# A transformer block on one core: fillers by a running count, last weights behind attention outputs, two more quads on VectorE, LayerNorm priorities

## The chip, the core and the metric

The kernel runs on one core of a Trainium2 chip. The core has five engines with an instruction stream each: TensorE (PE in the profile, its weight loads PEld), VectorE (DVE), ScalarE (ACT), GpSimd (POOL) and SyncE (SP), which here issues nearly all DMAs. The streams meet only at semaphores, and each engine takes its instructions in order. The metric is the device time of one execution in microseconds (us). Lower is better.

## The reference

One adaptive LayerNorm block over 2048 tokens of width 640: attention with 32 heads of width 20, then a gated product network of width 1536. All inputs are bf16.

```python
mod = (_silu(c) @ w_mod).reshape(c.shape[0], 6, 1, -1)
sa, ca, ga, sb, cb, gb = ...
h = _layernorm(x) * (1 + ca) + sa
x = x + ga * _A_ref(h, A_wqkv, A_wo)      # softmax(q k^T / sqrt(20)) v, 32 heads, then wo
h = _layernorm(x) * (1 + cb) + sb
x = x + gb * _B_ref(h, B_w_gate, B_w_up, B_w_down)   # ((h wg) * (h wu)) wd
```

The scores are 32 matrices of 2048 x 2048, so 134 million exponentials are taken.

## The kernel before

**A planner.** The Python code does not write the engines' programs by hand. It makes tasks (class `Task`) with an engine, an estimated duration, dependencies and a priority, plays them through an event loop (`Sched.run`, `step_engine`, `pick_pe`) and writes each engine's instructions in the order in which that loop started them. `emit_program` then adds the semaphore waits. The estimates therefore decide only the *order*; on the chip an instruction waits for its semaphores, and everything behind it on its engine waits too. A DMA's estimated landing is computed in `finish_issue`: bytes at `DMA_RATE_2` = 240 per ns, then `DMA_LAT` 1700 ns, `DMA_SLOW` 0.0015 ns per byte, and after 60 us `DMA_MARGIN`, unless the transfer is `firm`.

**Tiling.** Queries are cut into six chunks (`CHUNKS`: 512, 512 and four of 256). In each chunk eight items of four heads follow each other. The scores of an item are cut into units of 128 partitions x 512 columns; a head uses 32 rows of TensorE's array, so four heads run side by side (L1502). Most units go in groups of two through ScalarE's exponential (L1539) into the `PP` ring. The others are computed by VectorE, four units at a time, a *quad*: four evictions that write the score as bits of a bf16 (L1563), two masks (L1595, L1603) and a product on VectorE (L1600) or in four pieces on GpSimd (L1615). A quad's result has two terms, so its units pass twice through the product with V (L2165). `QUADS` says how many quads each item of each chunk has, 104 in all.

**End of an item** (`item_end_tasks`). The accumulated product is transposed by VectorE (L1695), a reciprocal is taken (L1700), the product with it (L1702) runs on GpSimd, a second VectorE transpose writes `OcT` (L1711), and DMAs on SP's queue place it in `Ocp` (L1723). `ENDP` is the priority of these VectorE steps for a chunk's last item; `END3` decides whether that item's product runs on VectorE.

**After a chunk** (`suffix(ci)`), beside the next chunk's attention: output projection from `Ocp` (`wo,Ocp`, L952; added to x at L1804), second LayerNorm (statistics L1821 and L1823 on VectorE, L1824 and L1826 on GpSimd, normalisation L1828), transposes of its result (L1866) with eviction into `h2T` (L1871), twelve rounds of gate and up (`h2T,stg`) with their product (L1932, L1939), and the down projection (`wd,hprod`, added at L2035). All these have lower standing on TensorE than scores. The LayerNorm steps have priority `LN2P` on VectorE, where smaller goes first: evictions have 1, a quad's evictions 0.8. The last chunk's suffix has nothing behind it to run beside: it is the tail. Its matmuls use the whole array (L948, L1844).

**FFN weights** come by DMA (L1907), gate and up 160 KB each for 128 of the 1536 columns. For the first five chunks they go through three buffers `stg`, in turn. For the last chunk, ten of the twelve pairs have buffers of their own (`stx`) in space that the queries held; the first `nsq` pairs wait for the last score of the fifth chunk (`sfx_done["qdead"]`), the others for the fourth chunk's leftovers (`first`).

**The running count.** `activity(t, area)` notes each matmul group's work, a transpose like any other matmul (2.37 units per ns of estimated duration). `recent(t)` is the sum over the last `HAM_W` = 3413.3 ns. `roll` sums the same work over windows that start at multiples of `HAM_W`; where one has less than `HAM_MIN` = 2550, `cold` is set, and `clk()` doubles TensorE's estimated durations.

**What TensorE does next** (`pick_pe`): scores, if they can go; else, with little recent work, other work ahead of its turn; else products with V; else other work; else a filler. The lines that the change touches:

```python
if sc.recent(t) < FILL_MIN and ring() >= RINGLOW and pick_x(t, True):
    return True
if sc.recent(t) < FILL_HARD and t > 20000 and do_fill(t):
    return True
```

A filler (`do_fill`, L2498) is four matmuls of 32 x 512 columns of the identity into a free PSUM bank; it needs such a bank, and its result is not used. `STAGE` holds thresholds of these choices by item.

Of the kernel before, what the change touches and what calls it, by code (L numbers as in the profile page):

```python
# [130 lines left out]
class Sched:  # L131

    def __init__(self):
        self.tasks = []
        self.order = {k: [] for k in ("sp", "act", "pe", "dve", "pool")}
        self.all = []
        self.free_at = {k: T0 for k in self.order}
        self.pend = {k: [] for k in self.order}
        self.readyl = {k: [] for k in self.order}
        self.t = 0.0  # L140
        self.n = 0
        self.progress = 0
# [5 lines left out]
        self.ham_w = 0  # L148
        self.ham_act = 0.0
# [12 lines left out]
        self.lk_last = None  # L162
# [45 lines left out]
        heapq.heappush(self.pend[task.eng], (t, task.seq, task))  # L208

    def roll(self, t):  # L210
        w = int(t // HAM_W)
        while self.ham_w < w:
            self.cold = self.ham_act < HAM_MIN
            if self.cold:
                self.ncold += 1
            self.ham_act = 0.0
            self.ham_w += 1

    def activity(self, t, area):
        self.roll(t)  # L220
        self.ham_act += area
        self.hist.append((t, area))
        self.acts.append((t, area))

# [121 lines left out]
def emit_program(nc, sched, nsem_dma=56):  # L346
# [121 lines left out]


CHUNKS = ((0, 512), (512, 512), (1024, 256), (1280, 256), (1536, 256), (1792, 256))  # L470
QUADS = ((0, 4, 3, 3, 3, 4, 4, 4), (3, 5, 2, 4, 3, 4, 4, 4), (2, 1, 2, 1, 2, 1, 2, 1), (2, 1, 2, 1, 2, 1, 2, 1), (2, 2, 1, 2, 2, 2, 1, 2), (2, 1, 2, 2, 2, 1, 2, 0))
SPLITJ = 1
QHALF = ((0, 0), (0, 0))
TB_GATE = 2
# [75 lines left out]
NTERM = 2  # L550

STAGE = {
    0: {"FILL_MIN": 4190.746, "D_LATE": 16, "HOLD": 95, "PVMIN": 2, "XBACK": 0, "PVMAX": 14, "PVCAP": 12, "STEAL_GAP": 200, "XDPRIO": 1.343, "PVTOL": 249, "D_RES": 74, "LKTOL": 300.0, "EAGER": 9, "PV_KEEP": 2, "X_HALF": 0.0, "X_LATE": -179.96, "TPRIO": 0.75},
    1: {"FILL_MIN": 4712.6, "PV_KEEP": 2, "LKTOL": 200.7},
    2: {"DL": 0.376, "PVMAX": 4},
    3: {"HOLD": 124.6},
    5: {"STEAL_GAP": 310.6, "X_HALF": -32.3, "HOLD": 67.9},
    7: {"DL": 0.501, "D_RES": 40, "D_LATE": 17, "STEAL_GAP": 186.7},
    8: {"PV_KEEP": 3, "LKTOL": 0},
    9: {"X_HALF": -45.3},  # L560
    10: {"PVMIN": 1, "PV_KEEP": 3, "X_HALF": 68.7, "X_LATE": 186.7, "D_LATE": 21},
    11: {"DL": 0.443, "EAGER": 4, "FILL_MIN": 3731.3, "X_HALF": 38.6},
    12: {"DL": 0.459},
    13: {"DL": 0.417, "PVCAP": 17, "X_LATE": 44.2},
    15: {"D_RES": 41, "D_LATE": 22, "X_LATE": -177.3},
    16: {"X_LATE": -8.0, "EAGER": 6},
    19: {"DL": 0.471, "FILL_MIN": 4603.8, "XBACK": 0, "EAGER": 5},
    20: {"DL": 0.391, "HOLD": 136.1},
    21: {"XBACK": 0, "X_LATE": -47.9, "PV_KEEP": 2},
    22: {"X_HALF": -100, "X_LATE": -44.0},  # L570
    23: {"STEAL_GAP": 63.5, "X_HALF": 45.7, "HOLD": 124.7},
    24: {"DL": 0.464},
    25: {"DL": 0.549},
    26: {"DL": 0.411, "X_LATE": 65.8, "PVMAX": 3, "EAGER": 8},
    27: {"DL": 0.473},
    29: {"HOLD": 38.5, "PVMIN": 2, "LKTOL": 11.4},
    30: {"D_RES": 7, "PVMAX": 4, "X_HALF": -29.6},
    31: {"X_LATE": -186.8, "X_HALF": 32.8, "HOLD": 130.6},
    32: {"EAGER": 5, "D_LATE": 14, "HOLD": 153.7, "LKTOL": 269.4},
    33: {"DL": 0.442, "XBACK": 4, "PV_KEEP": 1},  # L580
    34: {"X_LATE": 5.0},
    35: {"X_LATE": 15.7},
    36: {"DL": 0.524, "EAGER": 3},
    38: {"HOLD": 43.6},
    42: {"HOLD": 47.1, "XBACK": 0},
    45: {"EAGER": 9, "PVTOL": 185.1},
}
XHALF = 1
STG_G0, STG_G, XC_G = 12, -10, -20
# [12 lines left out]
def build_kernel(nc, A_x, A_wqkv, A_wo, B_x, B_w_gate, B_w_up, B_w_down, c, w_mod, out):  # L602
# [184 lines left out]
    def ring():  # L787
        return len(pPs[0].free) + len(pPs[1].free)
# [961 lines left out]
    def suffix(ci):  # L1750
# [112 lines left out]
        for k in range(0 if tail and SPLITJ else KD):  # L1863
# [13 lines left out]
            if tail and T_SPLIT:  # L1877
# [20 lines left out]
        for fc in range(FT):  # L1898
            use_x = tail and fc < nsx
            wbuf, dm = [], []  # L1900
            for w_, wv in enumerate((wgv, wuv)):
                cell = {}
                if use_x:
                    cell["t"] = stx[fc][:, w_, :, :]

                def f(e, wv=wv, fc=fc, cell=cell):
                    return e.dma_start(cell["t"], wv[:, :, fc * 128:(fc + 1) * 128])  # L1907
# [461 lines left out]
    def pick_pe(t):  # L2369
# [204 lines left out]
```

## Time and profile before

| what | value |
|---|---|
| runs | 812.86, 808.64, 812.66 us; median 812.66 |
| profiled execution | 814.7 us, span 812.9 us |
| mean granted TensorE clock | 0.991 |
| VectorE masks L1595 | 104, 713 ns each |
| quad evictions L1563 | 416, 682 ns each |
| quad products on VectorE L1600 | 39, 1265 ns each |
| quad products on GpSimd L1615 | 260 pieces, 1155 ns each |
| product at an item's end on GpSimd L1702 | 512 columns 1136 ns (16), 256 columns 657 ns (31) |
| fillers after the first 20 us, L2498 | 128 matmuls in 32 fillers |

The span runs from the first to the last instruction. Busy times of an engine count overlapping instructions once, so the mean of one instruction can be longer than busy time by count. A matmul's end is modelled. "Idle before" names what ended the wait.

### The profile page before, as it was taken

The numbers are of one execution on the slowest core, as the hardware profiler recorded it, in microseconds if no ns is written. First come the engines' busy times: TensorE is split into PE (matmuls) and PEld (weight loads), VectorE is DVE, ScalarE is ACT, GpSimd is POOL, SyncE is SP. The second block draws the span as 40 slices with busy tenths as digits, with TensorE's granted clock in tenths as the row PEclk, the third lists the DMA queues.
The fourth block names the chain that finished last, engine by engine and source line by source line (L and its number), as shares of the span: only waits on it lengthen the run. The fifth ranks groups of instructions, "written<-read, shape, count | busy, mean of one in ns | idle before, by whom it ended". The sixth has DMA issues, their size and how long they took to land.

```text
span 812.9 us, 34131 instructions
## 1 busy us (share of the span) xinstructions
PE 796.0 (98%) x14867; PEld 345.3 (42%) x14867; DVE 685.9 (84%) x1337; ACT 767.0 (94%) x851; POOL 360.6 (44%) x374
## 2 busy tenths in 40 slices
PE   8999999999999999999999999999999999999998
PEld 4434424332233222233343334445555555554567
DVE  7888868899999799998988878976798989799564
ACT  6899999999999799999999999999999999999941
POOL 2346344563374343444446334453546555652200
PEclk9999999999999699999999999999999999999999
DMA  9743222213241242201300232100432054444410
GB/s 298 238 121 81 59 58 65 58 33 109 73 103 34 82 114 62 49 4 46 71 17 11 49 79 56 38 23 23 97 86 54 26 118 102 98 95 97 95 36 18
DMA packets 136387, 60.49 MB, mean 74 GB/s; under 512 B 100703, under 2 KB 136239, under 8 KB 136239
## 3 DMA queue, kind: packets, MB, share of 16 engines
q1 hardware_dynamic: 135311, 57.16, 27.4%
q8 instruction: 118, 1.93, 1.1%
q10 hardware_dynamic: 928, 1.15, 0.4%
q14 instruction: 30, 0.25, 0.1%
HBM read 46.70 MB, written 8.99 MB: 69 GB/s over the span
## 4 chain that ended last, share of the span: by engine, by line
PE 49%; ACT 40%; issue 6%; DVE 3%; DMA 1%; SPq 0%; ACTq 0%; DVEq 0%
ACT PP L1539 40%; PE ps_all L1502 17%; PE ps_all L952 13%; PE ps_all L2165 11%; PE ps_all L1212 3%; PE ps_all L948 3%; DMA wm<-in_w_mod_dram 1%; DVE DB L1563 1%; PE ps_all L1109 1%; DVE DSS L1595 1%; PE ps_all L1866 1%; PE ps_all L1148 1%; DVE DSS L1603 0%; PE ps_all L2498 0%; DVE KPA L1221 0%
## 5 line engine op out<-in xcount | busy, mean ns | idle before, releaser
L1539 ACT ACTIVATE PP<-ps_all 128x1024 bf16<-128x1024 f32 x816 | 751.0, 1157 | 7.4 <-PE ps_all L1502 6.5
L1615 POOL TENSOR_TENSOR DSS<-DB,DSS 128x512 bf16<-128x512 bf16 x260 | 295.5, 1155 | 325.1 <-DVE DSS L1603 273.4
L1502 PE MATMUL ps_all<-QT,KT 32*128 32x256 bf16 (+2 forms) x3136 | 324.0, 308 | 9.5 <-ACT PP L1539 6.1
L1563 DVE TENSOR_SCALAR DB<-ps_all 128x512 int16<-128x512 f32 x416 | 277.4, 682 | 55.1 <-PE ps_all L1502 52.8
L1502 PEld LDWEIGHTS ps_all<-QT,KT 32*128 32x128 bf16 x3136 | 89.7, 92 | 239.4 <-ACT PP L1539 202.9
L2165 PE MATMUL ps_all<-PP,Vf 128*32 128x256 bf16 (+2 forms) x2520 | 165.8, 313 | 0.8 <-DVE DB L1563 0.4
L952 PE MATMUL ps_all<-h2T,stg 128*32 128x256 bf16 (+2 forms) x2272 | 122.8, 303 | 0.2 <-DVE DB L1563 0.2
L2165 PEld LDWEIGHTS ps_all<-PP,Vf 128*32 128x32 bf16 (+1 forms) x2520 | 49.6, 94 | 83.1 <-issue 76.0
L2165 PE MATMUL ps_all<-DSS,Vf 128*32 128x256 bf16 (+1 forms) x1232 | 84.6, 317 | 0.1
L1595 DVE TENSOR_SCALAR DSS<-DB 128x2048 int16<-128x2048 int16 x104 | 74.2, 713 | 0.5
L1603 DVE TENSOR_SCALAR DSS<-DB 128x2048 int16<-128x2048 int16 x104 | 72.8, 700 | 0.6 <-PE ps_all L2165 0.6
L952 PEld LDWEIGHTS ps_all<-h2T,stg 128*32 128x32 bf16 x2272 | 50.9, 96 | 28.1 <-issue 21.4
L952 PE MATMUL ps_all<-wd,hprod 128*32 128x320 bf16 (+1 forms) x1348 | 62.4, 281 | 0.0
L1702 POOL TENSOR_TENSOR OTn<-OT,invT 128x256 bf16<-128x256 f32 (+1 forms) x47 | 38.5, 820 | 53.0 <-DVE invT L1700 53.0
L1600 DVE TENSOR_TENSOR DSS<-DB,DSS 128x2048 bf16<-128x2048 bf16 x39 | 49.3, 1265 | 0.1
L2165 PEld LDWEIGHTS ps_all<-DSS,Vf 128*32 128x32 bf16 (+1 forms) x1232 | 29.5, 95 | 24.6 <-issue 14.2
L952 PEld LDWEIGHTS ps_all<-wd,hprod 128*32 128x32 bf16 x1348 | 31.1, 96 | 16.0 <-issue 10.3
L952 PE MATMUL ps_all<-wV,hT 128*32 128x160 bf16 x1280 | 37.3, 234 | 0.5 <-DVE hT L1117 0.2
L1695 DVE STREAM_TRANSPOSE OT<-ps_all 128x256 f32<-128x256 f32 (+2 forms) x49 | 25.7, 524 | 13.2 <-PE ps_all L2165 12.9
L1212 PE MATMUL ps_all<-hT,wq 128*32 128x512 bf16 x375 | 33.2, 397 | 0.0
L1212 PE MATMUL ps_all<-hT,wk 128*32 128x512 bf16 (+1 forms) x360 | 32.8, 382 | 0.2 <-DVE Vf L1301 0.2
L952 PE MATMUL ps_all<-wo,Ocp 128*32 128x320 bf16 (+1 forms) x664 | 30.7, 280 | 0.3
(131 smaller groups left out, 524.6 us busy)
## 6 DMA issues: line engine op xcount, KB each, us to landing
stg<-in_B_w_gate_dram SPq DMA_DIRECT2D x62, 160.0 KB
stg<-in_B_w_up_dram SPq DMA_DIRECT2D x62, 160.0 KB
KT<-k_rows SPq DMA_DIRECT2D x112, 32.0 KB
wm<-in_w_mod_dram SPq DMA_DIRECT2D x3, 800.0 KB
x<-in_A_x_dram SPq DMA_DIRECT2D x7, 320.0 KB
k_rows<-KPA SPq DMA_DIRECT2D x16, 128.0 KB
QT<-q_rows SPq DMA_DIRECT2D x32, 64.0 KB
wd<-in_B_w_down_dram SPq DMA_DIRECT2D x1, 1920.0 KB
```

The lines of the kernel that those rows point to most:

```text
L952: return lambda e, b: e.matmul(ps[32 * x:32 * x + 32, b, c0 + o:c0 + o + w], lhs()[:, 32 * x:32 * x + 32], rhs() if w == n else rhs()[:, o ...
L1212: f = [lambda e, b_, k=k, x=x: e.matmul(ps[x:x + min(32, w - x), b_, :], wx[:, k, r0 + x:r0 + min(x + 32, w)], hT[tc][:, k, :], tile_posit ...
L1502: ems.append(lambda e, i=i, kt=kt: e.matmul(dstf()[:, i * u.n:(i + 1) * u.n], KT[32 * u.s:32 * u.s + 32, u.j, kt * 128:(kt + 1) * 128], QT ...
L1539: return e.activation(PPs[g % 2][:, cellp["p"], 0:nu * 512], ps[:, b0:b0 + nu, :].rearrange("p b c -> p (b c)"), AFT.Exp, scale=ESCALE)
L1563: return e.tensor_scalar(DBl[st_["slot"]][:, x * 512:(x + 1) * 512], bank(cell["b"]), EBIAS, 0.0, op0=ALU.add, op1=ALU.max)
L1595: return e.tensor_scalar(DSl[st_["ss"][0]][:, :], DBl[st_["slot"]][:, :], 0x7F, 0x3F00, op0=ALU.bitwise_and, op1=ALU.bitwise_or)
L1600: return e.tensor_tensor(d, DBl[st_["slot"]][:, :].bitcast(BF16), d, ALU.mult)
L1603: return e.tensor_scalar(DSl[st_["ss"][1]][:, :], DBl[st_["slot"]][:, :], 0x7F80, 2, op0=ALU.bitwise_and, op1=ALU.bitwise_or)
L1615: return e.tensor_tensor(d, DBl[st_["slot"]][:, x * w:x * w + w].bitcast(BF16), d, ALU.mult)
L1695: t1 = Task("dve", n * 1.1 + 70, lambda e: e.transpose(OT[:, 0:n], ps[:, item_info[it]["bank"], 0:n].rearrange("p (b q r) -> p b r q", q=3 ...
L1702: f3 = lambda e: e.tensor_tensor(OTn[:, 0:n].rearrange("p (b c r) -> p b r c", c=32, r=2), OT[:, 0:n].rearrange("p (b r c) -> p b r c", c= ...
L2165: ems.append(lambda e, i=i, kt=kt, stt=stt, stp=stp: e.matmul(ps[32 * s:32 * s + mc, bk, 0:u.n], Vf[:, (kt * H + 4 * u.j + s) * VW:(kt * H ...
```

## The change

- `FILL_HARD` goes from 0 to 3000, and its branch is moved ahead of the `FILL_MIN` branch. `roll` keeps four sets of windows, shifted by a quarter of `HAM_W`; any of them can set `cold`, and only the first clears it.
- The fourth chunk's `QUADS` sum goes from 12 to 14, so there are 106 quads.
- Staged and last weights are counted by the planner with 0.95 instead of 2 times their bytes (`STG_B`), and `DMA_MARGIN` is halved. The bytes moved are the same.
- The last chunk's `stx` loads also wait for the fifth chunk's last `Ocp` DMAs (`oc_ready`).
- `LN2P` goes from 1.0 to 0.85; `END3` from 0 to 1.
- The transposes into `h2T` wait for the buffer before the matmul and not only before the eviction, and in the last two chunks for `first`.
- `STAGE` has other numbers in most items (the first item's are the same in another order).

```diff
-DMA_MARGIN = 1000.0
+DMA_MARGIN = 500.0
...
     def roll(self, t):
-        w = int(t // HAM_W)
-        while self.ham_w < w:
-            self.cold = self.ham_act < HAM_MIN
...
+        for i in range(4):
+            w = int((t - i * HAM_W / 4) // HAM_W)
+            while self.ham_w[i] < w:
+                low = self.ham_act[i] < HAM_MIN
+                if low:
+                    self.ncold += 1
+                if i == 0 or low:
+                    self.cold = low
+                self.ham_act[i] = 0.0
+                self.ham_w[i] += 1
...
-QUADS = (..., (2, 1, 2, 1, 2, 1, 2, 1), (2, 2, 1, 2, 2, 2, 1, 2), (2, 1, 2, 2, 2, 1, 2, 0))
+QUADS = (..., (2, 2, 1, 2, 2, 2, 1, 2), (2, 2, 1, 2, 2, 2, 1, 2), (2, 1, 2, 2, 2, 1, 2, 0))
...
-FILL_HARD = 0.0
+FILL_HARD = 3000.0
...
-LN2P = 1.0
+LN2P = 0.85
...
-ENDP, END3, P_POW = 0.4, 0, -1.0
+STG_B = 0.95
+ENDP, END3, P_POW = 0.4, 1, -1.0
...
-    1: {"FILL_MIN": 4712.6, "PV_KEEP": 2, "LKTOL": 200.7},
-    2: {"DL": 0.376, "PVMAX": 4},
-    3: {"HOLD": 124.6},
-    5: {"STEAL_GAP": 310.6, "X_HALF": -32.3, "HOLD": 67.9},
+    2: {"DL": 0.376},
+    4: {"HOLD": 53.4},
+    5: {"HOLD": 88.7, "STEAL_GAP": 176.5},
...
-            r = Round(mms, list(t_xn2), after, pr(True), gate=gate(n), name=f"h2T{ci}.{k}")
+            r = Round(mms, t_xn2 + (first if alt else bd.get("h2T", [])), after, pr(True), gate=gate(n),
+                      name=f"h2T{ci}.{k}")
...
-                t = dma("sp", 2 * 128 * KD * 128 * 2, f, sfx_done["qdead"] if use_x and fc < nsq else first if use_x else kp_use if ci == 0 else [], prio=16 + ci + .01 * fc,
+                t = dma("sp", int(STG_B * 128 * KD * 128 * 2), f,
+                        (sfx_done["qdead"] if fc < nsq else first) + oc_ready[(NC - 2, CHUNKS[-2][1] // 128 - 1)] if use_x else
+                        kp_use if ci == 0 else [], prio=16 + ci + .01 * fc,
...
+        if sc.recent(t) < FILL_HARD and t > 20000 and do_fill(t):
+            return True
         if sc.recent(t) < FILL_MIN and ring() >= RINGLOW and pick_x(t, True):
             return True
-        if sc.recent(t) < FILL_HARD and t > 20000 and do_fill(t):
-            return True
```

More of the change, by code (lines that the diff above doesn't have):

```diff
@@ L147, in __init__ @@
         self.every = []
-        self.ham_w = 0
-        self.ham_act = 0.0
+        self.ham_w = [0, -1, -1, -1]
+        self.ham_act = [0.0] * 4
         self.cold = True
@@ L210, in roll @@
     def roll(self, t):
-        w = int(t // HAM_W)
-        while self.ham_w < w:
-            self.cold = self.ham_act < HAM_MIN
[L214 to L217, printed above, removed]
+        for i in range(4):
[8 more added lines that the diff above has]
+                self.ham_w[i] += 1
     def activity(self, t, area):
         self.roll(t)
-        self.ham_act += area
+        for i in range(4):
+            self.ham_act[i] += area
         self.hist.append((t, area))
@@ L470 @@
 CHUNKS = ((0, 512), (512, 512), (1024, 256), (1280, 256), (1536, 256), (1792, 256))
-QUADS = ((0, 4, 3, 3, 3, 4, 4, 4), (3, 5, 2, 4, 3, 4, 4, 4), (2, 1, 2, 1, 2, 1, 2, 1), (2, 1, 2, 1, 2, 1, 2, 1), (2, 2, 1, 2, 2, 2, 1, 2), (2, 1, 2, 2, 2, 1, 2, 0))
+QUADS = ((0, 4, 3, 3, 3, 4, 4, 4), (3, 5, 2, 4, 3, 4, 4, 4), (2, 1, 2, 1, 2, 1, 2, 1), (2, 2, 1, 2, 2, 2, 1, 2), (2, 2, 1, 2, 2, 2, 1, 2), (2, 1, 2, 2, 2, 1, 2, 0))
 SPLITJ = 1
@@ L570 @@
-    22: {"X_HALF": -100, "X_LATE": -44.0},
-    23: {"STEAL_GAP": 63.5, "X_HALF": 45.7, "HOLD": 124.7},
+    0: {"D_LATE": 16, "PVMIN": 2, "X_LATE": -179.96, "XDPRIO": 1.343, "LKTOL": 300.0, "FILL_MIN": 4190.746, "HOLD": 95, "TPRIO": 0.75, "PVTOL": 249, "EAGER": 9, "X_HALF": 0.0, "XBACK": 0, "D_RES": 74, "PVCAP": 12, "PVMAX": 14, "STEAL_GAP": 200, "PV_KEEP": 2},
+    2: {"DL": 0.376},
+    4: {"HOLD": 53.4},
+    5: {"HOLD": 88.7, "STEAL_GAP": 176.5},
+    7: {"DL": 0.501},
+    9: {"LKTOL": 115.1},
@@ new lines @@
+    10: {"X_HALF": 5.8},
+    11: {"DL": 0.443, "EAGER": 4, "FILL_MIN": 3731.3, "X_HALF": 38.6},
+    12: {"DL": 0.459, "LKTOL": 438.4, "STEAL_GAP": 303.4, "EAGER": 10, "X_HALF": 21.8},
+    13: {"DL": 0.417, "FILL_MIN": 4496.3, "STEAL_GAP": 266.2, "X_HALF": 20.9},
+    15: {"LKTOL": 166.0, "PVMAX": 5, "EAGER": 10, "XBACK": 1},
+    16: {"PVCAP": 10, "PVMAX": 3, "EAGER": 10, "FILL_MIN": 5086.4},
+    17: {"X_HALF": -35.2},
+    18: {"EAGER": 3, "X_LATE": -36.1, "HOLD": 42.4, "PVMIN": 1},
+    19: {"DL": 0.471, "EAGER": 2, "X_HALF": 94.7},
@@ L572 @@
+    20: {"DL": 0.391},
+    21: {"EAGER": 6, "FILL_MIN": 4510.3, "X_HALF": 24.2, "D_LATE": 5},
+    22: {"PVMAX": 7, "X_HALF": 147.8, "EAGER": 9, "X_LATE": -21.9, "HOLD": 66.8},
+    23: {"HOLD": 124.7, "X_HALF": 14.5},
     24: {"DL": 0.464},
-    25: {"DL": 0.549},
+    25: {"DL": 0.549, "PV_KEEP": 3, "X_LATE": 36.2},
     26: {"DL": 0.411, "X_LATE": 65.8, "PVMAX": 3, "EAGER": 8},
-    27: {"DL": 0.473},
-    29: {"HOLD": 38.5, "PVMIN": 2, "LKTOL": 11.4},
-    30: {"D_RES": 7, "PVMAX": 4, "X_HALF": -29.6},
@@ L578 @@
[L578 to L586, printed above, removed]
+    27: {"DL": 0.473, "XBACK": 1, "HOLD": 186.0, "FILL_MIN": 3881.8, "X_LATE": -1.8},
+    28: {"X_HALF": 33.6, "FILL_MIN": 4310.0, "XBACK": 0},
@@ new lines @@
+    29: {"PVMAX": 7, "X_LATE": -9.2},
+    30: {"X_LATE": -109.9, "HOLD": 140.4, "XBACK": 1},
+    31: {"X_LATE": 202.7, "D_RES": 21},
+    32: {"PVCAP": 11, "X_HALF": -25.7, "X_LATE": 197.5},
+    33: {"DL": 0.442},
+    34: {"PVMIN": 5, "X_HALF": 27.8, "XBACK": 1},
+    35: {"X_HALF": -31.6, "PVMAX": 14},
+    36: {"DL": 0.524},
+    37: {"X_LATE": -50.4},
+    40: {"XBACK": 1, "HOLD": 36.3},
+    41: {"X_LATE": 52.1, "X_HALF": -52.1},
+    44: {"X_LATE": -66.5, "EAGER": 4, "D_RES": 10},
+    47: {"FILL_MIN": 5302.0},
@@ L587 @@
+    48: {"PVCAP": 14, "FILL_MIN": 3192.3},
 }
```

12 lines of the change are left out of this document (removed).

## The prediction

> **What bounds the kernel now.** I read the page first, then busy time by 20 us stretches, then 1 us stretches where the clock moves, then timelines of the staging queue and of the tail.
>
> ```profile
> span 812.9 us, 34131 instructions
> PE 796.0 (98%) x14867; PEld 345.3 (42%) x14867; DVE 685.9 (84%) x1337; ACT 767.0 (94%) x851; POOL 360.6 (44%) x374
> ACT  6899999999999799999999999999999999999941
> PEclk9999999999999699999999999999999999999999
> L1539 ACT ACTIVATE PP<-ps_all 128x1024 bf16<-128x1024 f32 x816 | 751.0, 1157 | 7.4 <-PE ps_all L1502 6.5
> ```
>
> ScalarE's 816 exponentials bound the kernel from about 40 to 780 us: 751.0 us busy, idle 7.4 us in all. 751.0/816 is 0.920 us each; five in a row take 4.52 us in the chain of waits, 0.904 each. The other engines matter only where they hold ScalarE up, or after its last exponential near 780 us. TensorE's 98% is modelled time; counting columns, its array is used for 0.55 to 0.68 of each 20 us between 40 and 780, so there is room.
>
> One digit stands out: clock and ScalarE dip in the fourteenth slice.
>
> ```profile
> 243.80:264.20 20.40, 19.82 (x209) 6.36 (x208) 20.17 (x41) 20.40 (x23) 10.12 (x12) 0.97 0.12 34
> 264.20:284.50 20.30, 20.30 (x184) 4.63 (x186) 15.06 (x25) 15.84 (x17) 7.17 (x7) 0.69 0.26 82
> 284.50:304.80 20.30, 19.98 (x280) 5.97 (x276) 19.23 (x33) 20.30 (x24) 8.16 (x8) 1.00 0.42 114
> ...
> 262.00:263.00 1.00, 0.63 (x7) 0.22 (x5) 1.00 (x3) 1.00 (x2) 0.00 (x0) 0.99 0.00 0
> 263.00:264.00 1.00, 1.00 (x6) 0.18 (x6) 1.00 (x3) 1.00 (x2) 0.56 (x1) 0.50 0.03 8
> 276.00:277.00 1.00, 1.00 (x13) 0.23 (x10) 1.00 (x2) 0.73 (x1) 0.33 (x1) 0.69 0.00 0
> ```
>
> (Columns: length, busy time of TensorE, weight loads, VectorE, ScalarE, GpSimd, then granted clock.) The clock falls at 262.98 (0.99 over that microsecond) and returns at 276.62 (0.69): 13.64 us at half. ScalarE is busy 15.84 of 20.30 us there and 20.40 and 20.30 of as much on both sides: **the dip costs 4.5 us**. The runs before are 812.86, 808.64 and 812.66: 4.1 us apart, so I read the middle one as a run without the dip.
>
> **The change, part by part.**
>
> *Fillers (FILL_HARD 0 to 3000, ahead of the other branch; four phases in `roll`).* I gave every matmul of N columns N units, a quarter of that if it uses 32 rows or columns, and summed over 3.41 us, the planner's window HAM_W. After 20 us the sum is under 3000 only around 66.6 to 67.8, at 203.1, and from 262.8 through the dip. So few fillers are added; one is four 512-column matmuls, 0.39 us in the timeline, on a TensorE with room. Ends: nothing gained (0) to the whole dip (4.5). I take 4.5: one filler's 512 lifts the last count ahead of the fall from 2859 to 3371, above the 3072 of a stretch that stayed warm (it ends at 201.5 us, a whole number of windows earlier). If TensorE had no room there, a filler would cost its 0.39 us, some 2 us for five.
>
> The sum counts transposes as work. Without them the stretch ahead of the fall counts 1835, and stretches of the same phase that stayed warm 2261 (723.7 us), 2432 and 2347. Both countings separate cold from warm, so this trace does not decide. [...]
>
> *Quads (fourth chunk 12 to 14).* The diff has two quads more, not four: eight units, four fewer ScalarE groups. Gain 4 x 0.904 = 3.6 us if VectorE can carry it. Its cost: eight evictions at 0.682, two masks at 0.713, two at 0.700: 8.3 us, and two products, 1.265 each on VectorE or 4 x 1.155 on GpSimd; at most 10.8.
>
> ```profile
> 491.00:585.00 94.00, 93.80 (x2070) 45.01 (x2066) 74.94 (x142) 94.00 (x104) 41.00 (x44) 1.00 0.20 48
> 585.00:680.00 95.00, 94.20 (x2311) 50.34 (x2302) 84.50 (x168) 94.88 (x105) 52.49 (x53) 1.00 0.31 72
> ```
>
> The fourth chunk's stretch has VectorE busy 74.94 of 94 us, 19 free; the fifth already has 14 quads, VectorE 84.50 of 95, and ScalarE lacks 0.12 us. So it fits. If VectorE were full, all 10.8 us would fall on the path, a loss of 7.2.
>
> *Weights in staging (STG_B 2 to 0.95, DMA_MARGIN 1000 to 500) and the last weights behind Ocp.* The planner puts a FFN round where it believes its weights have landed, and the attention output of the fifth chunk at SP's next turn.
>
> ```profile
> 687.27 0.31 DVE L1711 STREAM_TRANSPOSE OcT<-OTn 128x128 f32<-128x128 f32 x1
> 691.68 0.83 SPq L1907 DMA_DIRECT2D stx<-in_B_w_gate_dram  x1
> 692.56 2.99 SPq L1723 DMA_DIRECT2D Ocp<-OcT  x4
> ...
> 702.37 0.53 PE L952 MATMUL ps_all<-wo,Ocp 128*32 128x320 bf16 x12
> ...
> 731.57 0.63 SPq L1907 DMA_DIRECT2D stg<-in_B_w_up_dram  x1
> 733.83 0.46 PE L952 MATMUL ps_all<-h2Tt,stg 128*32 128x128 bf16 x12
> 743.06 0.45 PE L952 MATMUL ps_all<-h2Tt,stg 128*32 128x256 bf16 x12
> ```
>
> The output is ready at 687.58, but SP is in a run of stx loads until 692.5: 5.0 us late, and the output projection starts at 702.37. Later, FFN matmuls stop at 734.29 and resume at 743.06: 8.8 us, with seven fillers in them. The weights of that round were issued at 731.00 and 731.57, and the DMA share falls from 1.12 (733 to 734) to 0.32: they had landed by about 734.5. What held the round back was the place it was given, from a load counted at twice its bytes. A loaded stretch moves 228 to 260 GB/s, 0.63 to 0.72 us per 160 KB; the new figure is 0.65. What this is worth shows in the tail:
>
> ```profile
> 781.81 0.32 PE L952 MATMUL ps_all<-wd,hprodt 128*32 128x320 bf16 x4
> 783.49 4.12 PE L952 MATMUL ps_all<-wd,hprodt 128*32 128x320 bf16 x116
> 787.93 2.22 PE L952 MATMUL ps_all<-wd,hprodt 128*32 128x320 bf16 x60
> 790.08 5.76 PE L948 MATMUL ps_all<-h2Tc,stx 128*128 128x128 bf16 x100
> ```
>
> The whole down projection of the fifth chunk (4+12+116+60 = 192 matmuls) lies behind the last exponential, and the last chunk's gate and up rounds start only at 790.08, though their first tile was written by 784.84 (five evictions from 783.49, 1.35 us). Moved into the ScalarE-bound stretch it frees at most 790.08 - 784.84 = 5.2 us. It is 6.5 us of array time (192 x 80 units at 2370 per us); other matmuls use 0.15, 0.26 and 0.30 of the array at 720, 740 and 760 us against 0.34 to 0.37 in the fullest stretches, so 60 us hold about 6. Ends 0 and 5.2. I take 3.0, since the repairs give 5 and 8.8 us of head start, but some must queue behind scores.
>
> *Second LayerNorm sooner (LN2P 0.85), END3, h2T's wait on the matmul.* These reorder VectorE, GpSimd and TensorE inside the covered stretch. END3 moves five products (two of 1.136 us, three of 0.657 on GpSimd: 4.2 us) to VectorE at chunk ends; VectorE's one such row there is 0.30 us for 128 columns, so by columns 0.6 and 1.2 each, 4.2 us over 700. The moved wait keeps a transpose from holding a PSUM bank early; queued behind it are other FFN rounds of the same chunk, which wait for it anyway. I take 0; without ScalarE's cover it would be those 4.2.
>
> *Retuned STAGE table.* It changes which ready task goes first. Ends: a gain of what ScalarE still loses, 751.0 - 816 x 0.904 = 13.3 less the dip's 4.5, so 8.8; a loss if every stretch lost what 61.0 to 81.3 does, 0.51 per 20 us against some 2.5 now over 700: 15. I take 0.
>
> **Sum.** The profiled execution took 814.7 us (span 812.9). 814.7 - 4.5 - 3.6 - 3.0 = 803.6. It lies 2.0 above the median 812.66, so the forecast is **801.6**; its own range, 796 to 806, is the tail's ends and half the table's gain.
>
> **Rivals.** Half a percent, 4.1 us, is what a measurement can tell from no change.
>
> 1. *The dip stays, or another comes.* For: the count without transposes; banks are short there (VectorE 20.17 of 20.40 busy), and a filler needs one. Against: at 201.5 both counts agree and it is warm. 801.6 + 4.5 = 806.1.
> 2. *The tail keeps the down projection.* For: 0.55 to 0.60 of the array is used from 720 to 780 already, between scores each 0.9 us. Against: the 8.8 us hole. 801.6 + 3.0 = 804.6.
> 3. *The new order gives the gains back.* The table is worth about -11: 808.6 to 816.7, no change.
> 4. *Slower: TensorE waits for weights.* Place: the 60 staged rounds of five chunks. The planner now expects a pair 1.93 us sooner (0.5 margin, 2 x 0.717 of size). TensorE runs in order, so scores queue behind a round whose weights are late, and ScalarE waits for those. It has some 0.9 us of cover, one exponential. To lose 0.5% after gaining 11.1 it must idle 15.2 us, 0.25 a round: the deciding point is loads 1.15 us later than now planned. At 0.3 a round, 18 us: 819.6. Against: the lone pair issued at 738.10 and 738.66 stops moving by 741.0 (DMA share 1.11 then 0.04), and the new planning puts it at 738.66 + 0.40 + 0.65 + 1.70 + 0.23 + 0.50 = 742.1; the twelve from 723.14 drain by 734.3, planned 735.1. Neither is late.
>
> **Chances.** Forecast 0.50, first rival 0.15, second 0.13, third 0.08, fourth 0.14. Faster by over 0.5%: 0.50 + 0.15 + 0.13 = 0.78; within: 0.08; slower: 0.14. The range is 795 to 812: below it lies more of the table's gain than I count on (0.05), above it the fourth case.
>
> **What would show it.** Right: clock digits of 9 throughout, 812 exponentials with the mean interval kept; no hole of over 5 us in the fifth chunk's FFN matmuls; attention output issued within 2 us of its transpose; gate and up rounds of the last chunk starting some 5 us after the last exponential instead of 10. Wrong: a slice with clock under 0.9, ScalarE idle rows released by matmuls on staged weights, or VectorE full in the fourth chunk with ScalarE behind it.

## The result, and the profile after

The changed kernel took 807.02 us (median of 13 runs, 804.93 to 809.76) beside 812.72 (808.64 to 817.06, 13 runs) for the kernel before: ratio 0.9942, 95% interval 0.9922 to 0.9963. The forecast was 801.6. The direction is right; the gain is 5.7 us where 11.1 were forecast. The profiled execution took 806.1 us. One execution of the kernel before (1274 us) and one of experiment 7 (1269 us), both at full clock, stand far apart from all others and are left out of the figures.

First the page of the changed kernel: span, busy time, slices of ScalarE and the clock, and the exponentials (line numbers are higher in the changed file: L1548 was L1539).

```profile
span 804.3 us, 34189 instructions
PE 786.4 (98%) x14875; PEld 345.9 (43%) x14875; DVE 688.5 (86%) x1355; ACT 762.8 (95%) x847; POOL 361.9 (45%) x373
ACT  6899899999999999999999999999999999998951
PEclk9999999999999999999999999999999999999999
L1548 ACT ACTIVATE PP<-ps_all 128x1024 bf16<-128x1024 f32 x812 | 746.8, 1145 | 7.5 <-PE ps_all L1511 5.2
```

There are 812 exponentials instead of 816, and the 6 in the clock digits is gone. Yet ScalarE is idle 7.5 us before its exponentials, as much as before (7.4): a new wait must have come for the one that went. Busy time by stretches finds it (columns as before: length, TensorE, weight loads, VectorE, ScalarE, GpSimd, granted clock, DMA share, GB/s).

```profile
264.20:284.50 20.30, 20.14 (x257) 5.56 (x258) 17.79 (x29) 20.30 (x23) 14.19 (x14) 1.00 0.53 157
491.80:583.30 91.50, 91.20 (x2088) 44.82 (x2088) 80.16 (x153) 91.50 (x102) 50.32 (x50) 1.00 0.18 44
...
724.00:744.10 20.10, 17.96 (x428) 9.76 (x420) 13.01 (x29) 16.87 (x19) 12.14 (x12) 0.92 0.77 158
```

The last of these stretches in the kernel before:

```profile
724.00:744.10 20.10, 19.58 (x466) 9.64 (x470) 18.51 (x36) 19.98 (x23) 7.75 (x8) 1.00 0.67 150
```

The stretch of the old dip has clock 1.00 and ScalarE busy for all of its 20.30 us (15.84 before). The fourth chunk carries its two further quads with ScalarE full (91.50 of 91.50). But at 724 to 744, where the kernel before had no dip (19.98 of 20.10, clock 1.00), ScalarE is busy 16.87 of 20.10 and the clock is 0.92.

Where the time went is read best from the same exponential in both traces, since ScalarE bounds the kernel (start times in us, instruction by instruction):

| point | before | after | after is ahead by |
|---|---|---|---|
| 250th exponential | 253.49 | 253.40 | 0.09 |
| 300th, past the old dip | 304.69 | 299.18 | 5.51 |
| first of the fourth chunk | 496.62 | 491.68 | 4.94 |
| first of the fifth chunk | 592.06 | 583.30 | 8.76 |
| last | 778.86 | 774.79 | 4.07 |
| end of the span | 812.88 | 804.31 | 8.57 |

So the dip gives 5.4 in these two executions, the quads 3.8, the tail 4.5; from the fifth chunk's first exponential to the last one 4.7 are given back. In TensorE's timeline of the tail, the down projection of the fifth chunk now starts ahead of the last exponential:

```profile
772.66 0.52 PE L961 MATMUL ps_all<-wd,hprodt 128*32 128x160 bf16 x12
778.57 0.32 PE L961 MATMUL ps_all<-wd,hprodt 128*32 128x320 bf16 x4
779.07 0.32 PE L961 MATMUL ps_all<-wd,hprodt 128*32 128x320 bf16 x4
779.70 1.54 PE L961 MATMUL ps_all<-wd,hprodt 128*32 128x320 bf16 x40
781.18 2.74 PE L957 MATMUL ps_all<-h2Tc,stx 128*128 128x128 bf16 x46
```

Only 4 + 4 + 40 = 48 of 192 matmuls are left behind it (all 192 before), and the last chunk's gate round starts at 781.18 instead of 790.08. The attention output is issued 0.15 us after its transpose (679.54 and 679.70; 5.0 us before), its projection starts at 686.88 instead of 702.37.

Most of what is given back is one wait at 729 us, for weights of the fifth chunk's gate and up rounds, which run beside the last chunk's exponentials. First the queue of SP, then TensorE, then ScalarE (in brackets the idle time ahead and its inferred end), then 1 us stretches:

```profile
723.68 0.53 SPq L1917 DMA_DIRECT2D stx<-in_B_w_up_dram  x1
724.25 0.53 SPq L1917 DMA_DIRECT2D stx<-in_B_w_gate_dram  x1
724.81 0.53 SPq L1917 DMA_DIRECT2D stx<-in_B_w_up_dram  x1
725.38 0.53 SPq L1917 DMA_DIRECT2D stx<-in_B_w_gate_dram  x1
725.95 0.53 SPq L1917 DMA_DIRECT2D stg<-in_B_w_gate_dram  x1
726.53 0.56 SPq L1917 DMA_DIRECT2D stg<-in_B_w_up_dram  x1
727.13 2.03 SPq L1917 DMA_DIRECT2D stx<-in_B_w_up_dram  x1
```
```profile
728.99 0.29 PE L961 MATMUL ps_all<-h2Tt,stg 128*32 128x256 bf16 x4
731.42 0.46 PE L961 MATMUL ps_all<-h2Tt,stg 128*32 128x256 bf16 x12 [2.14 <-DVE DSS L1612]
```
```profile
732.25 1.02 ACT L1548 ACTIVATE PP<-ps_all 128x1024 bf16<-128x1024 f32 x1 [2.07 <-PE ps_all L1511]
```
```profile
732.00:733.00 1.00, 1.00 (x28) 0.72 (x24) 0.00 (x0) 0.76 (x1) 1.00 (x2) 0.68 1.18 253
733.00:734.00 1.00, 1.00 (x21) 0.46 (x18) 0.23 (x1) 0.55 (x2) 1.00 (x2) 0.50 1.11 202
734.00:735.00 1.00, 1.00 (x20) 0.30 (x8) 0.79 (x2) 0.75 (x1) 1.00 (x2) 0.50 0.08 17
735.00:736.00 1.00, 1.00 (x23) 0.61 (x20) 0.00 (x0) 0.74 (x1) 0.93 (x1) 0.62 0.04 10
```

The pair of staged weights (`stg`) is issued at 725.95 and 726.53 behind four of the last chunk's loads (`stx`). The matmuls at 731.42 stand in TensorE's order ahead of the next scores; TensorE is idle 2.14 us ahead of them. The profile names a VectorE operation, but experiment 1 moves only loads and the wait goes, and in experiment 2 the profile names this pair's second load. ScalarE waits 2.07 us, and a window of half clock follows (0.32 + 0.50 + 0.50 + 0.38 of those four microseconds lost, 3.4 us at half), in which ScalarE is idle again. Experiment 6 tells the two apart.

### The profile page after: what moved, and what is told of

It is laid out like the page before. It is cut to its first block, busy times and chain, and to the rows that moved or that the text cites. A ratio compares the mean times of both kernels' runs of the same rounds, so it can differ in the third digit from the quotient of the medians.

```text
span 804.3 us, 34189 instructions
## 1 busy us (share of the span) xinstructions
PE 786.4 (98%) x14875; PEld 345.9 (43%) x14875; DVE 688.5 (86%) x1355; ACT 762.8 (95%) x847; POOL 361.9 (45%) x373
## 3 DMA queue, kind: packets, MB, share of 16 engines
q8 instruction: 118, 1.93, 1.0%
## 4 chain that ended last, share of the span: by engine, by line
PE 60%; ACT 24%; DVE 9%; issue 4%; DMA 2%; SPq 1%; ACTq 0%; DVEq 0%
ACT PP L1548 24%; PE ps_all L1511 20%; PE ps_all L961 18%; PE ps_all L2177 14%; DVE DB L1572 3%; PE ps_all L957 3%; PE ps_all L1221 2%; DMA wm<-in_w_mod_dram 1%; DVE DSS L1612 1%; DVE DSS L1604 1%; DVE DSS L1609 1%; SPq L1732 1%; PE ps_all L2510 1%; PE ps_all L1118 1%; PE ps_all L1157 1%
## 5 line engine op out<-in xcount | busy, mean ns | idle before, releaser
L1548 ACT ACTIVATE PP<-ps_all 128x1024 bf16<-128x1024 f32 x812 | 746.8, 1145 | 7.5 <-PE ps_all L1511 5.2
L1624 POOL TENSOR_TENSOR DSS<-DB,DSS 128x512 bf16<-128x512 bf16 x264 | 300.1, 1157 | 335.3 <-DVE DSS L1612 276.6
L1572 DVE TENSOR_SCALAR DB<-ps_all 128x512 int16<-128x512 f32 x424 | 283.6, 683 | 60.7 <-PE ps_all L1511 58.3
L1511 PE MATMUL ps_all<-QT,KT 32*128 32x256 bf16 (+2 forms) x3136 | 319.1, 307 | 7.0 <-ACT PP L1548 4.1
L1511 PEld LDWEIGHTS ps_all<-QT,KT 32*128 32x128 bf16 x3136 | 89.2, 92 | 229.2 <-ACT PP L1548 191.5
L2177 PE MATMUL ps_all<-PP,Vf 128*32 128x256 bf16 (+2 forms) x2504 | 164.0, 311 | 0.6 <-DVE Vf L1310 0.6
L1711 POOL TENSOR_TENSOR OTn<-OT,invT 128x256 bf16<-128x256 f32 (+1 forms) x42 | 34.8, 829 | 34.2 <-DVE invT L1709 34.2
L2177 PEld LDWEIGHTS ps_all<-DSS,Vf 128*32 128x32 bf16 (+1 forms) x1264 | 31.3, 96 | 20.1 <-issue 8.5
L1221 PE MATMUL ps_all<-hT,wq 128*32 128x512 bf16 x375 | 31.4, 382 | 0.0
L961 PEld LDWEIGHTS ps_all<-wV,hT 128*32 128x32 bf16 x1280 | 24.0, 96 | 15.4 <-issue 8.4
```

Source lines behind the costliest of these rows:

```text
L961: return lambda e, b: e.matmul(ps[32 * x:32 * x + 32, b, c0 + o:c0 + o + w], lhs()[:, 32 * x:32 * x + 32], rhs() if w == n else rhs()[:, o ...
L1221: f = [lambda e, b_, k=k, x=x: e.matmul(ps[x:x + min(32, w - x), b_, :], wx[:, k, r0 + x:r0 + min(x + 32, w)], hT[tc][:, k, :], tile_posit ...
L1511: ems.append(lambda e, i=i, kt=kt: e.matmul(dstf()[:, i * u.n:(i + 1) * u.n], KT[32 * u.s:32 * u.s + 32, u.j, kt * 128:(kt + 1) * 128], QT ...
L1548: return e.activation(PPs[g % 2][:, cellp["p"], 0:nu * 512], ps[:, b0:b0 + nu, :].rearrange("p b c -> p (b c)"), AFT.Exp, scale=ESCALE)
L1572: return e.tensor_scalar(DBl[st_["slot"]][:, x * 512:(x + 1) * 512], bank(cell["b"]), EBIAS, 0.0, op0=ALU.add, op1=ALU.max)
L1624: return e.tensor_tensor(d, DBl[st_["slot"]][:, x * w:x * w + w].bitcast(BF16), d, ALU.mult)
```

## The experiments

Two ways of editing were used. Most keep the order of one of the two kernels and change or move a few entries of it, so that the rest stays the same. Planning again with one constant undone gives another order everywhere; two of these stand at the end. For the kernel before, each batch has its own runs.

**1. The last chunk's later loads behind all staged ones** (order after).

```diff
+    put_behind(lambda n: n in {f"stx5.{fc}.{w}" for fc in range(5, 10) for w in range(2)}, "stg4.11.1")
```

> The changed kernel with its planned order kept, except that the last ten loads of the last chunk's weights (pairs 5 to 9) stand on SP's queue behind all of the fifth chunk's staged weights. Theory 'queue': the 2.1 us that TensorE stood still at 729.3 us came from those loads going ahead of and between the fifth chunk's own; the wait goes, with it the empty clock window behind it, ScalarE loses under 0.5 us between 720 and 744 instead of 3.3; median some 3 us under 807.0, about 804. Rival 'too early': the round was put where its weights cannot be there, since a staging buffer comes free too late whatever stands in the queue; TensorE still waits about 2 us and the time stays at 807.

Measured: 801.64 us (800.78 to 802.26, 6 runs, each with mean clock 1.000), ratio 0.9873 (0.9853 to 0.9893), span 800.5. The stretch of the wait:

```profile
724.00:744.10 20.10, 20.07 (x526) 11.33 (x518) 16.05 (x36) 20.10 (x23) 14.64 (x14) 1.00 0.44 98
```

ScalarE is full, TensorE has no wait over 0.5 us from 715 to 770. From the fifth chunk's first exponential to the last one it takes 187.3 us against 191.5. The queue was the cause; the moved loads, now issued from 748 to 755, delay nobody.

**2. The same ten loads as large packets** (order after; they fetch rows of x in 1280-byte packets, so the weights of those five pairs are left out).

```diff
+                    if ci == NC - 1 and 5 <= fc < 10:
+                        return e.dma_start(cell["t"].rearrange("p k n -> p (k n)"), xv[:, fc, :])
```

> The changed kernel with its order kept; the last ten loads for the last chunk (pairs 5 to 9) fetch rows of x, 128 packets of 1280 bytes, in place of weights in 640 packets of 256 bytes: the weights of these pairs are left out. Bytes and number of DMAs on SP are the same. Theory 'transfer': the staged weights were late because the DMA engines worked off 12 loads of small packets; the 2.1 us wait at 729 us goes or falls under 0.7, about 802 to 803. Rival 'issue': SP needs 0.53 us or more for each DMA it issues (planned 0.40), whatever is fetched, and its queue slips; TensorE still waits 1.5 us or more, about 806.

Measured: 803.54 us (803.26 to 804.19, 4 runs), ratio 0.9910 (0.9880 to 0.9941).

```profile
730.11 0.46 PE L961 MATMUL ps_all<-h2Tt,stg 128*32 128x256 bf16 x12 [1.08 <-DMA stg<-in_B_w_up_dram]
```

Half of the wait is left, 1.08 us of 2.14, and here the profile names the staged load. Neither theory alone holds. Issue is a part: each load of weights holds SP for some 0.53 us or more where the planner counts 0.40, and the pair's second load is issued 0.8 us sooner behind the large packets (725.72 for 726.53). The transfers are another: from that issue to the matmuls it takes 4.39 us instead of 4.89 (730.11 - 725.72 and 731.42 - 726.53). The clock stays at 1.00: the wait of 1.08 us did not bring a half-clock window in any of the four runs.

**3. The same move in the order before**, with the same lines.

> The kernel before with the same move on SP's queue: pairs 5 to 9 of the last chunk behind the fifth chunk's staged weights, TensorE's order untouched. Theory 'place': before the change TensorE did not wait for these weights, its rounds merely stood late in its order (8.8 us hole at 734 to 743 us); nothing moves, 811.4 and 808.3 in the runs at full clock. Rival 'data': earlier weights let the rounds go earlier; the hole closes and the tail loses some of its 8 us of down projection, 2 us or more faster.

Measured: 818.31 us (816.11 to 820.91, 6 runs), ratio 1.0091 (1.0061 to 1.0121): both theories missed. SP's queue and TensorE near the end:

```profile
766.01 0.53 SPq L1907 DMA_DIRECT2D stx<-in_B_w_gate_dram  x1
766.58 0.53 SPq L1907 DMA_DIRECT2D stx<-in_B_w_up_dram  x1
767.15 1.78 SPq L1907 DMA_DIRECT2D stg<-in_B_w_gate_dram  x1
768.98 0.67 SPq L1907 DMA_DIRECT2D stg<-in_B_w_up_dram  x1
769.69 2.97 SPq L1723 DMA_DIRECT2D Ocp<-OcT  x4
```
```profile
774.61 0.96 PE L948 MATMUL ps_all<-wo,Ocp 128*128 128x320 bf16 x3 [5.22 <-DMA Ocp<-OcT]
```

In that order the last staged loads come so late that the moved ones (759.6 to 767.1) delay the attention output of the last items: TensorE waits 5.22 us for it with scores behind, and ScalarE 5.37. It is the same kind of loss at another place: a run of weight loads ahead of a transfer that TensorE's order already counts on.

**4. Transposes ahead of the dip issued three times** (order before; the copies write the same values).

```diff
+    for t in sc.order["pe"]:
+        if t.name[:5] == "h2T0." and 258700.0 <= t.start < 260200.0:
+            t.emits = t.emits * 3
```

> The kernel before with its order kept; the eight transposes at 261 to 262 us are issued three times each, 16 matmuls of 128 x 128 more, 2048 units of the planner's count, more than the doubled scores bring. Theory 'transposes count': the clock no longer falls at 263, about 809 like the doubled scores. Theory 'transposes do not count': the fall stays, median about 812.7 or up to 1 us more, clock 0.991 in most runs.

**5. Scores ahead of the dip issued twice** (order before, same form).

> The kernel before with its order kept; the score groups from 258.5 to 263.5 us are issued twice, some 14 matmuls of 32 x 512 columns more. Both theories of the count: the stretch ahead of the fall is lifted to about 2800 without transposes and over 3800 with them, the clock no longer falls at 263; median from 812.7 to about 809, as in the runs of before without the fall (808.6 to 809.3). Rival 'another cause' (the stall itself, not the count): still about 812.7.

Measured: 809.68 us (808.57 to 812.95) and 810.53 (808.75 to 812.24), 12 runs each, beside 811.44 (29 runs) in that batch; ratios 0.9985 (0.9968 to 1.0002) and 0.9986 (0.9968 to 1.0005). The mean clock of the runs says more than the medians: 9 of the 29 runs before have 0.994 or less, none of these 24. The stretch of the dip, tripled transposes first, then doubled scores:

```profile
264.20:284.50 20.30, 19.59 (x249) 5.87 (x245) 19.57 (x33) 20.06 (x23) 10.10 (x9) 1.00 0.42 134
```
```profile
264.20:284.50 20.30, 19.86 (x246) 5.72 (x243) 19.62 (x34) 20.30 (x23) 9.44 (x9) 1.00 0.40 131
```

Both keep the clock at 1.00 (0.69 before), transposes as well as scores: here they count as work for the clock. The tripled transposes' trace shows it by itself. The traces have the clock's changes whole multiples of 3.413 us apart, one window: it is at half for 13.65 us or four of them in the kernel before (262.98 to 276.63), for 3.41 or one in the changed kernel (732.36 to 735.77), and 732.36 lies 727.04 us or 213 of them behind that trace's first edge at 5.32. With the transposes tripled the clock is at half from 10.14 to 13.55 us, and whole windows from there end at 262.73 and 266.14. Between these two the prediction's sum is some 1440 without transposes and 4500 with them, and the clock stays up; the window that fell before the change, up to 262.98, has 1868 and 2892 by the same counting (matmuls shared between windows by their time). The medians, and the 20 of 29 runs above 0.994, also say that the dip is not in every run: removing it is worth 0.9 to 1.8 us, with intervals that reach 1.

**6. Scores doubled in the order after**, at 256 to 260 us.

> The changed kernel with its order kept; four score groups around 257 to 260 us are issued twice (the second writes the same values), 8 matmuls of 32 x 512 columns more, so that the running count without transposes does not go under about 2300 there. Theory 'transposes do not count': part of the changed kernel's half-clock windows lie at 260 us (count without transposes 1536, with them over 3000); they go, the mean granted clock over the runs rises by 0.001 or more, median 0.5 to 2 us lower, about 805.5. Rival 'transposes count': the clock never fell at 260; nothing changes but some 0.5 us more for the matmuls, 807 to 807.5.

Measured: 806.00 us (804.01 to 812.15, 12 runs), ratio 0.9939 (0.9918 to 0.9961), not told apart from the changed kernel's 0.9942. Two of 12 runs still have clock 0.994 or less (3 of 13 in the changed kernel). Falls at this place were no longer what it lost. Its profiled execution, at clock 1.000 throughout, has the wait of the changed kernel without the half-clock window:

```profile
730.62 0.46 PE L961 MATMUL ps_all<-h2Tt,stg 128*32 128x256 bf16 x12 [2.07 <-DVE DSS L1612]
```
```profile
731.44 7.47 ACT L1548 ACTIVATE PP<-ps_all 128x1024 bf16<-128x1024 f32 x8 [2.00 <-PE ps_all L1511]
```

From the fifth chunk's first exponential to the last one this execution takes 190.9 us: 3.6 more than experiment 1, and 0.6 less than the changed kernel's. So the wait itself is most of the loss, and the window behind it is worth some 0.6.

**7. The three new fillers at 65 us taken out** (order after).

```diff
+    gone = {id(t) for t in sc.order["pe"] if t.name == "fill" and 64000.0 < t.start < 67000.0}
```

> The changed kernel with its order kept, less the three fillers at 65 us, the only ones that it has and the kernel before has not at a like place. Theory 'fillers idle': the fall at 263 went because the rounds around it stand in another order, not by fillers; same time, 807 (804.9 at full clock), clocks as in the changed kernel. Rival 'fillers hold the clock': the sum at 66 us, 2722 before, falls under the bound again, one to three more half-clock windows in some runs, median 1 us or more slower.

Measured: 807.85 us (804.43 to 812.38, 11 runs), ratio 0.9960 (0.9935 to 0.9985). Eight of 11 runs have clock 0.994 or less, and none 1.000. The profiled one:

```profile
64.80:68.00 3.20, 2.67 (x28) 0.75 (x30) 2.94 (x7) 2.82 (x4) 1.72 (x2) 0.57 0.22 51
68.00:71.00 3.00, 3.00 (x37) 0.74 (x26) 2.10 (x5) 2.08 (x3) 1.65 (x2) 0.50 0.27 71
71.00:85.00 14.00, 14.00 (x161) 4.49 (x154) 7.12 (x14) 9.70 (x10) 2.21 (x2) 0.50 0.30 75
```

The clock is halved from 65.25 to 85.73 us, 20.5 us or six windows of 3.41, and ScalarE is busy 2.08 of 3.00 and 9.70 of 14.00 us; in the changed kernel the clock of these stretches is 1.00 and ScalarE is full. So three fillers hold the clock at this place, in this execution. In the median the kernel is not told apart from the changed one (0.9960 and 0.9942, intervals overlap).

**8. As 1, and two late query transfers put ahead at 89 us** (four attention output writes go behind them).

```diff
+    put_behind(lambda n: n == "Ocp0.1", "QT4.0")
```

> The changed kernel with the last chunk's late loads moved as in a_stx_late, and on SP's queue two loads of QT ahead of four Ocp writes at 85 us. Theory: scores waited 0.6 to 1.7 us at 91 us for QT, and ScalarE 0.8 to 1.9 us with them; the wait shrinks by what SP can issue earlier, 1 to 2 us; 800.5, against 801.64. Rival: the loads wait for the writes of q anyway; no change, 801.6.

Measured: 801.89 us (801.14 to 804.26, 6 runs), ratio 0.9894 (0.9866 to 0.9923): the wait of 1.70 us for the transfer that experiment 1 shows at 91.31 is gone from TensorE's timeline, but the time is that of experiment 1.

**9 and 10. 144 matmuls of the down projection more, under cover or in the tail** (experiment 1's order). In 9 those ahead of the last score are issued twice, in 10 the 48 behind it four times.

```diff
+    for t in pe[:last]:
+        if t.name[:4] == "dn4.":
+            t.emits = t.emits * 2
```

> The kernel with the last weights' loads moved back (801.6 us), where the 144 down projection matmuls of the fifth chunk that lie ahead of the last score are each issued twice (the accumulated down projection of that chunk is changed by it). They are 5.5 us of TensorE time (40 of them took 1.54 us in the tail, 38.5 ns each). Theory 'cover' (the tail's gain comes from 144 matmuls that now lie behind ScalarE's work, and the array has room for them): no change, 801.6 to 802.4, ScalarE without holes from 750 to 765. Rival 'no room' (the array is full between the scores, my second rival's reason): scores come late, ScalarE waits for them, and up to 5.5 us come on top: 804 to 807.

> The same kernel, where instead the 48 down projection matmuls behind the last score are issued four times each: 144 more matmuls again, now in the tail (the down projection of that chunk's second tile is changed by it). Theory 'the tail is bound by TensorE's order': 144 x 38.5 ns = 5.5 us on top, 806.5 to 807.5; then putting 144 matmuls under cover is worth about what the tail was shortened by (4.5). Rival 'the tail waits for VectorE' (evictions and sums between the gate and up rounds): part of the matmuls falls into waits that are there anyway, under 3 us on top: 802 to 804.6.

Measured: 806.92 us (804.88 to 810.20) and 807.21 (805.50 to 810.43), 10 runs each; ratios 0.9937 (0.9910 to 0.9963) and 0.9944 (0.9914 to 0.9974); spans 804.9 and 806.2 beside 800.5. In the tail they cost nearly their TensorE time: from the last exponential to the end it takes 34.4 us for 29.5, 4.9 for 5.5 (the rest of the 5.7 us of span lies ahead of the fifth chunk), so the tail is in the main bound by TensorE's order. But under cover they cost 4.4, nearly as much. Experiment 1, then 9:

```profile
760.00:765.00 5.00, 5.00 (x160) 3.45 (x160) 0.49 (x1) 4.76 (x6) 0.00 (x0) 1.00 0.37 82
765.00:770.00 5.00, 5.00 (x163) 3.40 (x164) 2.03 (x6) 4.81 (x6) 0.00 (x0) 1.00 0.12 38
```
```profile
760.00:765.00 5.00, 5.00 (x164) 3.50 (x156) 0.49 (x1) 3.74 (x4) 0.00 (x0) 1.00 0.42 96
765.00:770.00 5.00, 5.00 (x157) 3.58 (x153) 0.49 (x1) 3.56 (x4) 0.00 (x0) 1.00 0.07 16
```

The first 144 matmuls leave ScalarE 4.76 and 4.81 of 5.00 us; the next 144 leave 3.74 and 3.56. The room that the change used there was just large enough, and it is used up.

**11. Planned again with 12 quads in the fourth chunk.**

```diff
-QUADS = (..., (2, 2, 1, 2, 2, 2, 1, 2), (2, 2, 1, 2, 2, 2, 1, 2), (2, 1, 2, 2, 2, 1, 2, 0))
+QUADS = (..., (2, 1, 2, 1, 2, 1, 2, 1), (2, 2, 1, 2, 2, 2, 1, 2), (2, 1, 2, 2, 2, 1, 2, 0))
```

> The changed kernel planned again with 12 quads in the fourth chunk as before; the whole order shifts with it. By the quads' term alone: four more exponentials, 3.6 us on top of the changed kernel's 807.0, 810.6, and the fourth chunk's exponentials take 3.6 to 3.8 us longer. Rival 'the order decides' (the numbers of STAGE fit one order only): the fourth chunk is longer by that, but the sum differs from it by several us in either direction, with new holes at other places, 805 to 818.

Measured: 814.22 us (811.65 to 816.54, 10 runs), ratio 1.0033 (1.0009 to 1.0058). From the fourth chunk's first exponential to the fifth's it takes 95.5 us instead of 91.6, 3.9 for four of them: the term is right. The sum is off by the order, and the place is the known one, with a longer wait:

```profile
736.68 1.04 PE L961 MATMUL ps_all<-h2Tt,stg 128*32 128x256 bf16 x16 [3.77 <-DMA stg<-in_B_w_up_dram]
```

SP issued ten `stx` loads around one staged pair from 720.3 to 730, the next pair only at 733.06 and 733.59. From the fifth chunk's first exponential to the last one it takes 194.5 us (after 191.5, experiment 1 187.3).

**12. Planned again with staged weights counted at twice their bytes** (`STG_B` 0.95 to 2.0).

> The changed kernel planned again with staged weights counted at twice their bytes (STG_B 2), the rest as changed. Theory 'planned too early': the planner now believes each load some 0.72 us longer, a pair 1.4 us, so it puts gate and up rounds later and the wait of 2.1 us at 731 goes: 801.5 to 804 if nothing else moves. Rival 'the order decides': the wait at that place may go, but the order is another one all through the kernel, and the time differs from 802 to 804 by new holes or colder stretches: 805 to 815. Rival 'queue': the order on SP, with the last weights among the staged ones, stays, and so does a wait of 1 to 2 us for staged weights there.

Measured: 806.97 us (805.56 to 809.01, 10 runs), ratio 0.9942 (0.9916 to 0.9967): the time of the changed kernel, made up otherwise. No wait over 0.5 us stands in TensorE's timeline from 715 to 770, and the last exponential starts at 771.71 instead of 774.79. But the tail keeps much of the down projection:

```profile
776.16 1.54 PE L961 MATMUL ps_all<-wd,hprodt 128*32 128x320 bf16 x40
778.02 3.17 PE L961 MATMUL ps_all<-wd,hprodt 128*32 128x320 bf16 x88
781.50 1.14 PE L961 MATMUL ps_all<-wd,hprodt 128*32 128x320 bf16 x28
782.57 5.76 PE L957 MATMUL ps_all<-h2Tc,stx 128*128 128x128 bf16 x100
```

From the last exponential to the end it takes 33.7 us, as before the change (34.0), where the changed kernel takes 29.5. In this plan the late counting avoids the wait and loses the head start; in the changed kernel's plan the early counting has the head start and the wait. Since the whole order differs, this shows one pair of plans, not the constant alone.

## Why the prediction was right in direction and wrong in size

The measured 807.02 lies within the stated 795 to 812, but above the forecast's own 796 to 806. That it is close to the first rival's 806.1 is chance: the dip that this rival keeps is gone.

**The step that failed** is rival 4's "Neither is late", by which weights in staging cost nothing. Of the two places that it tested in the trace before, one was a staged pair behind ten of the last chunk's loads:

```profile
723.14 0.47 SPq L1907 DMA_DIRECT2D stx<-in_B_w_gate_dram  x1
...
731.00 0.52 SPq L1907 DMA_DIRECT2D stg<-in_B_w_gate_dram  x1
```

The "planned 735.1" is the second load's issue on the chip with the planner's landing added: 731.57 + 0.40 + 0.65 + 1.70 + 0.23 + 0.50 = 735.05. So the landing was tested, and the issue was taken as given. But the eleven issues from 723.14 to 731.57 took 8.43 us, 0.77 each, where the planner counts 0.40. Before the change TensorE's timeline has no wait there: its rounds stood late (the hole of 8.8 us). The new planning puts the rounds soon after the planned landing, and the same ten loads (715.40 to 730.01) now stand ahead of and between the staged pairs. From 721.69 to 726.53 seven issues took 4.84 us where the planner counts 2.8, 2.0 us more, and TensorE waited 2.14 us.

The rival priced its mechanism as 0.25 us in each of 60 rounds, with 0.9 us of cover; it came in one round, above the cover. From the fifth chunk on 4.7 us were lost. Experiment 1 moves the ten loads, and 4.2 of them are back; 2 splits the wait into issue and small packets; 11 shows it again, longer. That experiment 1's 801.64 is what was forecast is luck and no proof of the terms: they were off in both directions.

| term, us | forecast | measured |
|---|---|---|
| dip | 4.5 | 5.4 in the two profiled executions; 2.0 in the medians, all falls together |
| quads | 3.6 | 3.8 |
| tail | 3.0 | 4.5 |
| weights in staging | 0 | -4.7 in the two profiled executions; -4.1 without the half-clock window (experiment 6's 190.9 beside 186.8 before) |

**The dip.** It is gone, as forecast, but the term was sized on an execution that had all of it, and then taken off a median that had only a part. Runs with mean clock 1.000 of the kernel before took 808.2 to 809.0 us, with 0.998 mostly 809.6 to 810.1, with 0.996 mostly 811 to 812.5: one window of half clock costs 1.2 to 1.5 us. Beside the changed kernel the median before, 812.72, lies 4.1 above its two lowest runs (808.64 and 808.68): that is what windows at several places took, of which experiments 4 and 5 get back 0.9 to 1.8 at 263 us. The changed kernel's median is 2.0 above its two runs at clock 1.000 (804.93 and 805.03). So falls account for 2.0 of the gain (4.06 - 2.04). What is left, 808.66 - 804.98 = 3.7, is 3.8 + 4.5 - 4.1 less 0.5 that has no place yet; in the profiled executions 0.6 is lost between the 300th exponential and the fourth chunk. Together this is the measured 5.7. The reason was partly wrong too: at 256 us both orders have one filler, so the new order of transposes and scores there keeps the clock. The fillers' work is at 65 us (experiment 7), where the count had its other low, 66.6 to 67.8.

**The count.** Transposes belong in it (4: the window with 1440 without them and 4500 with them kept the clock), so the first rival's ground falls. The bound was put between 2859, which fell, and 3072, which did not. Counted in the same units over the windows that each profiled execution's clock changes mark, from 10 us on, those that fell have up to some 3010 (at 737.68 us in experiment 7) and those that kept the clock some 2970 and more (at 227.40 us in experiment 9). So on this count the bound is near 3000, as far as modelled ends and missing records allow.

**Quads.** Right: ScalarE full with 14, and 3.9 us back with 12. **LayerNorm sooner, END3, the moved wait:** no loss seen by the trace, none was tried alone. **STAGE table:** taken at 0; no run tries it alone, and what it is worth stays open. **Small slips:** the hole at 734 to 743 us had five fillers in it (20 matmuls at L2498), not seven; and the 1.93 us by which a pair is expected sooner leave out `DMA_SLOW` on the smaller byte count, 0.0015 x 172032 = 0.26 us.

**Tail.** The mechanism is as forecast, the gain 4.5 of at most 5.2. The second rival doubted the room: 9 shows that there was room for these matmuls and for no more.

## What to carry to other kernels

Whether a transfer is late has to be tested from its place in the plan, issue and landing: list what stands ahead of it in its queue, with the issue time that the trace shows (0.53 to 0.77 us here) and not the one that a planner assumes (0.40). In an order made by estimates, one transfer that lands later than estimated stalls an engine that runs in order, scores and all (here TensorE for 2.14 us and ScalarE for 2.07); so transfers that nobody needs soon belong behind those that TensorE's next rounds need, and any replanning has to be searched for the next such wait. And look at the granted clock of all runs before a dip of one profiled execution is taken off a median.

## What was not expected of the hardware

A pause of 2.14 us was followed by a full half-clock window in the profiled execution of the changed kernel, a pause of 2.07 us at the same place by none in that of experiment 6, and one of 1.08 us by none in experiment 2. So the length of a pause alone does not settle whether the clock falls.

The traces show why the first two differ. In an execution the clock's changes stand whole windows of 3.413 us apart: in experiment 7's, 7.22 and 737.68 are 730.46 us or 214 windows apart. In the changed kernel's execution a window runs from 728.95 to 732.36 and holds the whole pause, 729.28 to 731.42; the sum in it is some 1500, and the clock falls. In experiment 6's the clock record begins at 6.33, so an edge lies 212 windows later, at 729.96, inside the pause from 728.55 to 730.62; the two windows share it, their sums are some 3130 and 3960, and the clock stays. The place of the windows differs from one profiled execution to another: counted back in whole windows, the first edge in the span lies 0.14 to 3.31 us behind its start (0.15 in the kernel before, 1.90 in the changed one, 2.92 in experiment 6). So the same kernel can get through a thin place at full clock in one run and not in another: the mean clock of the changed kernel's 13 runs goes from 0.992 to 1.000.

All six runs of experiment 1 and all four of experiment 2 had a mean clock of 1.000, the changed kernel 2 of 13: most of its windows went with the one wait. No run sets the place of the windows, so how often a given pause costs one is open.
